# A share of the first MLP beside attention: one weight group in the second batch, both from the third on, at another pace

## The chip, the cores and the metric

The kernel runs on one core of one Trainium2 chip. The metric is device time in microseconds (us) of one execution. Engines: PE is the matmul engine (PEld its weight loads), DVE, ACT and POOL are the vector, scalar and general engines, SP issues the DMAs.

## The reference

Attention with rotary positions over 4 batches of 8 heads, 576 tokens, head size 64, then two MLPs of width 2048 over the 2304 tokens of width 512. The second MLP differs only in its activation, `s * relu(h)**2 + b`.

```python
attn = softmax(rotate(q) @ rotate(k).T / 8); x = attn @ v
h = x @ w_in
g = np.where(h >= 1, h, np.where(h <= -1, 0.0, (h + 1) ** 2 / 4))
x = g @ w_out
```

## The kernel before, in words

Every product is made of three matmuls on operands split into a high and a low part (hi*hi, hi*lo, lo*hi).

**Attention** runs in units: 16 head pairs (4 per batch) of 9 units, 144 units numbered n from 0. A unit is a block of scores (L300), its negated maximum on DVE (L302), its exponential on ACT (L305), transposes on PE (L318, L330) with casts and subtractions (L320, L324), and, behind four of a pair's nine units, the product with v (`av`). Transposes run 2 units behind the scores, `av` 4 behind. One step of the loop at L518 traces, in this order: scores, loads and rope of the next pair, transposes, `av`, and then a share of other work, `do_fill`.

**That share** is the generator `beside` (L401). Its work items are (c, gi): c is a chunk of 288 tokens (two to a batch, 0 to 4 are done here, `FC`), gi one of two groups of four slices of the 2048 hidden columns of the first MLP (`set_a`, 8 of its 16 slices). One item is four h groups (12 matmuls of 128x288 and the activation `act1`, L162) and four y groups (12 matmuls, a copy `ys` at L421, a store to `yd`). After each group it yields 1.0. It first loads and splits x of the chunk (`split_x`, four loads, casts on ACT, subtractions on POOL) and then yields `LEAD` = 4 times without work. `run_fill` (L453) adds a budget per step, `RATE` = 0.67, and takes groups while the budget is positive. A new list of items is added when a batch's last pair is finished, at n = 39, 75 and 111 (L506 to L512): [(0,0), (1,0), (0,1), (1,1)], [(2,0), (2,1), (3,0), (3,1)] and [(4,0), (4,1)]. Together they are 80 groups and three LEADs, 92 yields. What is left at the end of attention is traced behind it (L524).

**Weights** come as 64-bit words. A slice (L101) has two halves of 512 columns: the first holds its part of w_in (used by h), the second its part of w_out (used by y). `half` (L107) turns one half into a high and a low part: a load (wraw), ACT L125, DVE L126 to L129, ACT L130 (the high part), POOL L88 twice two instructions (the low part). Its stages `wa` and `wm` have one buffer each, so conversions go one behind the other. `convert` (L446) makes the next of `pending`, which lists the 16 halves of `set_a` slice by slice; it is called when n % 4 == 0 from n = 8 to 32 (`CA`), 7 times, and then when n % 3 == 0 (`CB`). `beside` also makes what is missing: both halves ahead of a slice's h (L409).

**Behind attention** come five stages (L619 to L623). The first does chunks 5 to 7 with `set_a` and makes the 16 halves of `set_b`, the second needs those. Its x is split by `split_in(0)` (L556 to L559). The change touches no line of the stages.

The order on each engine is not the order of the trace alone: for the part up to L524 a planner with its own time model puts the instructions of each engine in order at build time (program order is the priority), and on the chip each engine runs its queue strictly in that order. In the stages PE's order is that of the program.

The lines that matter below:

```python
406            grp = set_a[gi * G1:(gi + 1) * G1]
409                while sl.made < 2:
410                    sl.half(wst, WB)
444    pending = [sl for sl in set_a for _ in range(2)]
488        if n > 5 and (n % CA == 0 if n < 36 else n % CB == 0):
515        run_fill(RATE)
```

Of the kernel before, what the change touches and what calls it, by code (L numbers as in the profile page):

```python
# [24 lines left out]
NP = H // 2  # L25
KD = DM // P
NF = DFF // P
GA = 8
G1 = 4
WB = 1  # L30
# [10 lines left out]
YP = 4  # L41
N2 = 464
LEAD = 4
RATE = 0.67
CA = 4
LT = 2
LA = 4
PB = 3
YB = 4
P2 = 100  # L50
CB = 3
M1 = False
CF = None
FC = 5
# [8 lines left out]
def kernel(ctx, tc, qq, kk, vv, tab, ww1, ww2, s, b, out):  # L63
# [26 lines left out]
    def split(dst_hi, dst_lo, src, hi_eng, lo_eng):  # L90
        if hi_eng is nc.scalar:
            nc.scalar.copy(dst_hi, src)  # L92
        else:
            hi_eng.tensor_copy(dst_hi, src)
        tt = pool_tt if lo_eng is nc.gpsimd else nc.vector.tensor_tensor
        tt(out=dst_lo, in0=src, in1=dst_hi, op=ALU.subtract)  # L96
# [39 lines left out]
    def accumulate(out_ps, terms, chain=None):  # L136

        n = len(terms)
        with ExitStack() as st:
            if chain in chains:  # L140
                st.enter_context(tc.issue_after(chains[chain]))
            for i, (l, r) in enumerate(terms):
                m = nc.tensor.matmul(out_ps, l, r, start=(i == 0), stop=(i == n - 1))  # L143
        if chain is not None:
            chains[chain] = m.ins

    def h_terms(w, xh, xl):
        t = []
        for c in range(KD):
            wh, wl = w[:, 0, c * P:(c + 1) * P], w[:, 1, c * P:(c + 1) * P]  # L150
            t += [(wh, xh[:, c, :]), (wh, xl[:, c, :]), (wl, xh[:, c, :])]
        return t

    def y_terms(ws, gs, d):
        t = []
        for w, (gh, gl) in zip(ws, gs):
            o = 512 + d * P
            wh, wl = w[:, 0, o:o + P], w[:, 1, o:o + P]
            t += [(wh, gh), (wh, gl), (wl, gh)]
        return t  # L160

    def act1(ps, n, pool, gpool, lo_eng):  # L162
        c = pool.tile([P, n], F32, tag="ac", name="ac", bufs=AC)
        nc.vector.tensor_scalar(out=c, in0=ps, scalar1=-1.0, scalar2=1.0, op0=ALU.max, op1=ALU.min)
        nc.scalar.activation(c, c, AF.Square, bias=0.5, scale=0.5)
        nc.vector.tensor_tensor(out=c, in0=c, in1=ps, op=ALU.max)
        gh = gpool.tile([P, n], F32R, tag="gh", name="gh")
        gl = gpool.tile([P, n], F32R, tag="gl", name="gl")
        split(gh, gl, c, nc.scalar, lo_eng)
        return gh, gl  # L170
# [14 lines left out]
    wst = ctx.enter_context(tc.tile_pool(name="wst", bufs=1, side="right", reuse_waits="tile"))  # L185
    set_a = [Slice(wpa, ww1, f) for f in range(GA)]
# [25 lines left out]
    def load_qk(i, nm, pieces=WHOLE):  # L212
        bb, hp = divmod(i, NP)
        t = att2.tile([P, 2, S], F32, tag="qkin", name=f"{nm}in", bufs=3)
        for c in pieces:
            nc.sync.dma_start(out=t[:, :, c], in_=(qq if nm == "q" else kk)[bb, hp, :, :, c])
        qk_in[nm, i] = t

    def load_v(i):
        bb, hp = divmod(i, NP)  # L220
        t = att2.tile([P, 5, 2, D], F32, tag="vin", name="vin")
        nc.sync.dma_start(out=t, in_=vv[bb, hp])
        v_in[i] = t
# [11 lines left out]
    def rope_pair(i, nm, eng, lo_eng, pieces=WHOLE):  # L235

        t = qk_in.pop((nm, i))
        hi, lo = t[:, 0, :].bitcast(F32R), t[:, 1, :].bitcast(F32R)
        for c in pieces:
            tt = pool_tt if eng is nc.gpsimd else nc.vector.tensor_tensor  # L240
            tt(out=t[:, :, c], in0=t[:, :, c], in1=tab_sb[:, :, c], op=ALU.mult)
            r = t[:, 1, c]
            tt(out=r, in0=t[:, 0, c], in1=r, op=ALU.add)
            if nm == "q":
                nc.scalar.activation(hi[:, c], r, AF.Copy, scale=0.125)
                nc.vector.scalar_tensor_tensor(out=lo[:, c], in0=r, scalar=0.125, in1=t[:, 0, c], op0=ALU.mult, op1=ALU.subtract)
            else:
                nc.scalar.copy(hi[:, c], r)
                pool_tt(out=lo[:, c], in0=r, in1=t[:, 0, c], op=ALU.subtract)
        parts_t[nm, i] = t  # L250
        if i > 0:
            stack(i, nm, 0)
            stack(i, nm, 1)
# [15 lines left out]
    def v_pair(i):  # L269
        t = v_in[i]  # L270
        vs = att2.tile([P, 5, 4, D], F32R, tag="vs", name="vs")
        nc.scalar.copy(vs[:, :, 0::3, :], t)
        pool_tt(out=vs[:, :, 1:3, :], in0=t, in1=vs[:, :, 0::3, :], op=ALU.subtract, dim=1)
        vs_t[i] = vs
# [117 lines left out]
    def split_x(c):  # L392
        xh = m1.tile([P, KD, N1], F32R, tag="xh", name="xh")
        xl = m1.tile([P, KD, N1], F32R, tag="xl", name="xl")
        for k in range(KD):
            xs = m2.tile([P, N1], F32, tag="xs", name="xs", bufs=1)
            nc.sync.dma_start(out=xs, in_=xd[k, :, c * N1:(c + 1) * N1])
            split(xh[:, k, :], xl[:, k, :], xs, nc.scalar, nc.gpsimd)
        return xh, xl

    def beside(work):  # L401
        x = split_x(work[0][0])
        for _ in range(LEAD):
            yield 1.0
        for n, (c, gi) in enumerate(work):
            grp = set_a[gi * G1:(gi + 1) * G1]
            gs = []
            for sl in grp:
                while sl.made < 2:  # L409
                    sl.half(wst, WB)  # L410
                ps = ps_f.tile([P, 512], F32, tag="bank", name="h")
                accumulate(ps[:, :N1], h_terms(sl.w, *x), CF)
                gs.append(act1(ps[:, :N1], N1, ac1, g1p, nc.vector if c < GE else nc.gpsimd))
                yield 1.0
            if n + 1 < len(work) and work[n + 1][0] != c:
                x = split_x(work[n + 1][0])
            for d in range(KD):
                ps = ps_f.tile([P, 512], F32, tag="bank", name="y")
                accumulate(ps[:, :N1], y_terms([sl.w for sl in grp], gs, d), CF)
                y = m2.tile([P, N1], F32, tag="ys", name="ys")  # L420
                nc.scalar.copy(y, ps[:, :N1])  # L421
                nc.sync.dma_start(out=yd[gi, d, :, c * N1:(c + 1) * N1], in_=y)
                yield 1.0
# [17 lines left out]
    units = [(i, k) for i in range(NPAIR) for k in range(9)]  # L441
    fill = []
    done = 0.0
    pending = [sl for sl in set_a for _ in range(2)]

    def convert():  # L446
        while pending:
            sl = pending.pop(0)
            if sl.made < 2:
                sl.half(wst, WB)  # L450
                break

    def run_fill(budget):  # L453
        nonlocal done
        done += budget
        while fill and done > 0:
            try:
                done -= next(fill[0])
            except StopIteration:
                fill.pop(0)  # L460
        if not fill:
            done = 0.0
# [9 lines left out]
    def do_load(n):  # L472
        if n < len(units):
            i, k = units[n]
            if i + 1 < NPAIR:
                if k == 0:
                    load_qk(i + 1, "k")
                elif k == 1:
                    rope_pair(i + 1, "q", nc.gpsimd, nc.vector)
                elif k == 3:  # L480
                    rope_pair(i + 1, "k", nc.gpsimd, nc.gpsimd)
                elif k == 5:
                    load_v(i + 1)
                elif k == 7:
                    v_pair(i + 1)
                    if i + 2 < NPAIR:
                        load_qk(i + 2, "q")
        if n > 5 and (n % CA == 0 if n < 36 else n % CB == 0):
            convert()

    def do_t(n):
# [8 lines left out]
    def do_av(n):  # L500
        if n >= LA:
            i, k = units[n - LA]
            if k in AVS:
                av(i, *AVS[k])
            if k == 8:
                finish_pair(i, *rbs.pop(i))  # L506
                if (i + 1) % NP == 0 and i // NP < B - 1:
                    c = 2 * (i // NP)
                    order = [(c, 0), (c + 1, 0), (c, 1), (c + 1, 1)] if c == 0 else [(c, 0), (c, 1), (c + 1, 0), (c + 1, 1)]
                    order = [o for o in order if o[0] < FC]  # L510
                    if order:
                        fill.append(beside(order))  # L512

    def do_fill(n):
        run_fill(RATE)

    acts = {"q": do_qk, "l": do_load, "t": do_t, "a": do_av, "f": do_fill}
    for n in range(len(units) + LA):  # L518
        with ExitStack() as st:
# [156 lines left out]
```

## Time and profile before

| | us |
|---|---|
| three runs: median (lowest to highest) | 1220.44 (1219.37 to 1221.54) |
| the profiled execution: its time | 1221.28 |
| its span, first to last instruction | 1219.5 |
| PE busy in the span | 1111.2 (91%) |
| DVE, ACT, POOL busy | 790.0, 606.7, 602.6 |
| mean granted clock of PE | 0.977 |

How to read it: the span is cut into stretches below. In each, the busy time of an engine is set against the stretch, and where PE is not busy the waits and the chain say for whom it waits. PE's granted clock is a mean over the stretch between two levels, 1.2 GHz (0.5) and 2.4 GHz (1.0).

### The profile page before, as it was taken

Reading aid. Unit: us, or ns where it says so; the run is one execution under the profiler, and the core shown is the slowest. Engines: PE = TensorE matmul, PEld = TensorE weight load, DVE = VectorE, ACT = ScalarE, POOL = GpSimd, SP = SyncE. Lnnn points to the kernel's source line nnn. Section 1 sums busy time; section 2 is a strip of 40 time slices with the busy share of each in tenths; the row PEclk is TensorE's granted clock in tenths of the full one; section 3 lists DMA queues with packets and bytes.
Section 4 is the critical chain, followed back from the end, with each engine's and each line's share of the span. In section 5 each row is a group of like instructions: output and inputs, shape, how many; then the busy total and the mean of one; then the engine's idle time right before and its main releaser. Section 6 shows DMA issues by size and latency. Waiting matters only on the chain.

```text
span 1219.5 us, 19127 instructions
## 1 busy us (share of the span) xinstructions
PE 1111.2 (91%) x6628; PEld 1029.7 (84%) x6628; DVE 790.0 (65%) x1363; ACT 606.7 (50%) x1315; POOL 602.6 (49%) x778
## 2 busy tenths in 40 slices
PE   2987778859999999999979989999999999999998
PEld 2676677749998999999979889999888889988887
DVE  4787888868898777467766676677863333434443
ACT  3786667747877776455443444444443233322221
POOL 6878776875644301256677888466641101110100
PEclk9899889989999999999989999999999999999999
DMA  8766654535554401243334545442421101212210
GB/s 234 199 183 180 184 160 127 178 118 167 164 145 133 119 30 60 87 136 114 113 100 147 157 144 157 141 130 85 157 69 62 32 32 63 83 43 63 71 61 34
DMA packets 75840, 142.09 MB, mean 117 GB/s; under 512 B 12000, under 2 KB 49376, under 8 KB 75744
## 3 DMA queue, kind: packets, MB, share of 16 engines
q1 hardware_dynamic: 75744, 140.88, 39.0%
q8 instruction: 52, 0.85, 0.3%
q14 instruction: 44, 0.36, 0.1%
HBM read 90.70 MB, written 26.54 MB: 96 GB/s over the span
## 4 chain that ended last, share of the span: by engine, by line
PE 57%; POOL 13%; DVE 9%; DMA 8%; issue 7%; ACT 5%; SPq 1%; POOLq 0%; ACTq 0%; DVEq 0%
PE hps L143 21%; PE yps L590 7%; PE yps L589 7%; PE yps L591 7%; PE av L143 4%; PE sc L143 4%; PE y L143 3%; POOL wm L88 3%; POOL w L88 3%; PE tp L318 2%; DMA xs<-xd 2%; POOL xl L88 2%; POOL kin L88 2%; DMA qs<-qin 2%; PE h L143 2%
## 5 line engine op out<-in xcount | busy, mean ns | idle before, releaser
L143 PE MATMUL hps<-xh,w 128*128 128x464 f32 (+5 forms) x1216 | 347.1, 350 | 8.6 <-ACT w L130 6.1
L88 POOL TENSOR_TENSOR xl<-xs,xh 128x232 fp32r<-128x232 f32 (+5 forms) x168 | 127.0, 780 | 282.4 <-ACT xh L92 282.2
L143 PEld LDWEIGHTS hps<-xh,w 128*128 128x128 f32 x1216 | 223.2, 189 | 24.6 <-ACT w L130 6.4
L589 PE MATMUL yps<-gh,w 128*128 128x464 f32 (+5 forms) x608 | 213.7, 351 | 9.3 <-ACT yo L596 5.8
L590 PE MATMUL yps<-gl,w 128*128 128x464 f32 (+5 forms) x608 | 212.9, 350 | 0.8 <-DVE gl L96 0.7
L591 PE MATMUL yps<-gh,w 128*128 128x464 f32 (+5 forms) x608 | 212.7, 350 | 0.0
L143 PE MATMUL hps<-xl,w 128*128 128x464 f32 (+5 forms) x608 | 212.4, 349 | 0.0
L88 POOL TENSOR_TENSOR wm<-wm,w 128x256 f32<-128x256 f32 x128 | 116.6, 932 | 149.3 <-ACT w L130 66.2
L143 PE MATMUL sc<-kh,qs 128*128 128x288 f32 x320 | 102.2, 334 | 43.7 <-ACT p L305 26.9
L175 DVE TENSOR_TENSOR ar<-ar,hps 128x464 f32<-128x464 f32 (+1 forms) x80 | 50.6, 632 | 132.7 <-ACT ar L174 132.7
L302 DVE TENSOR_REDUCE nm<-sc 128x1 f32<-128x576 f32 x144 | 108.0, 751 | 39.9 <-PE sc L143 38.8
L589 PEld LDWEIGHTS yps<-gh,w 128*128 128x128 f32 x608 | 114.9, 189 | 19.9 <-ACT yo L596 8.1
L590 PEld LDWEIGHTS yps<-gl,w 128*128 128x128 f32 x608 | 114.9, 189 | 8.8 <-DVE gl L96 1.3
L143 PEld LDWEIGHTS hps<-xl,w 128*128 128x128 f32 x608 | 114.9, 189 | 7.6
L591 PEld LDWEIGHTS yps<-gh,w 128*128 128x128 f32 x608 | 115.0, 189 | 7.5
L305 ACT ACTIVATE p<-sc,nm 128x576 f32<-128x576 f32 x144 | 106.8, 744 | 18.1 <-DVE nm L302 13.2
L143 PEld LDWEIGHTS sc<-kh,qs 128*128 128x128 f32 x320 | 64.0, 200 | 52.8 <-ACT p L305 34.2
L324 DVE TENSOR_TENSOR ptl<-tp,pth 128x512 fp32r<-128x512 f32 x134 | 90.4, 682 | 27.1 <-ACT pth L320 26.4
L174 ACT ACTIVATE ar<-hps 128x464 f32<-128x464 f32 (+1 forms) x80 | 44.2, 553 | 124.7 <-PE hps L143 124.4
L88 POOL TENSOR_TENSOR w<-wm,wa 128x256 fp32r<-128x256 f32 x128 | 99.4, 794 | 0.0
L318 PE MATMUL tp<-ident,p 128*128 128x128 f32 x576 | 90.0, 283 | 7.5 <-DVE ptl L324 6.1
L96 DVE TENSOR_TENSOR gl<-ac,gh 128x288 fp32r<-128x288 f32 (+3 forms) x112 | 75.5, 675 | 28.6 <-ACT gh L92 27.5
(85 smaller groups left out, 2287.7 us busy)
## 6 DMA issues: line engine op xcount, KB each, us to landing
wraw<-in_ww SPq DMA_DIRECT2D x64, 512.0 KB, 3.7
kh<-kin SPq DMA_DIRECT2D x64, 144.0 KB, 2.7
qs<-qin SPq DMA_DIRECT2D x64, 144.0 KB, 2.6
qin<-in_q SPq DMA_DIRECT2D x15, 576.0 KB, 5.1
kin<-in_k SPq DMA_DIRECT2D x15, 576.0 KB, 3.9
xs<-y1d SPq DMA_DIRECT2D x32, 232.0 KB, 2.5
xs<-xd SPq DMA_DIRECT2D x40, 144.0 KB, 2.4
yd<-ys SPq DMA_DIRECT2D x40, 144.0 KB, 1.9
```

Source lines behind the costliest of these rows:

```text
L88: nc.gpsimd.tensor_tensor(out=out[c], in0=in0[c], in1=in1[c], op=op)
L96: tt(out=dst_lo, in0=src, in1=dst_hi, op=ALU.subtract)
L143: m = nc.tensor.matmul(out_ps, l, r, start=(i == 0), stop=(i == n - 1))
L174: nc.scalar.activation(r, ps, AF.Relu)
L175: nc.vector.tensor_tensor(out=r, in0=r, in1=ps, op=ALU.mult)
L302: nc.vector.tensor_reduce(out=nm, in_=sc[:, :, :288], axis=AX.XY, op=ALU.max, negate=True)
L305: nc.scalar.activation(p, sc[:, :, :288], AF.Exp, bias=nm, scale=1.0, accum_out=sums_t[i][:, col:col + 1])
L318: nc.tensor.transpose(v[:, c, :], p_t[i, k][:, c * P:(c + 1) * P], ident)
L324: nc.vector.tensor_tensor(out=lo, in0=v, in1=hi, op=ALU.subtract)
L589: nc.tensor.matmul(acc, wh, gh, start=f == 0, stop=False)
L590: nc.tensor.matmul(acc, wh, gl, start=False, stop=False)
L591: nc.tensor.matmul(acc, wl, gh, start=False, stop=last)
```

## The change

Five things. The lists of the items become [(0,0), (1,0)] at n = 39, [(1,1), (0,1), (2,0), (2,1), (3,0), (3,1)] at n = 75 and [(4,0), (4,1)] at n = 111: the same ten items, the two of group 1 for the first batch's chunks moved from the first list to the second. The pace is 0.55 a step up to n = 75 and 0.95 from n = 76. From n = 36 on a half is converted every 5 steps, not every 3. `pending` now has, for each group of four slices, their four first halves and then their four second halves. And `beside` makes only the first half ahead of an h, and the second halves ahead of the group's y.

```diff
-RATE = 0.67
-CB = 3
+CB = 5
...
             for sl in grp:
-                while sl.made < 2:
+                while sl.made < 1:
                     sl.half(wst, WB)
...
                 x = split_x(work[n + 1][0])
+            for sl in grp:
+                while sl.made < 2:
+                    sl.half(wst, WB)
             for d in range(KD):
...
-    pending = [sl for sl in set_a for _ in range(2)]
+
+    pending = [sl for gi in range(GA // G1) for _ in range(2) for sl in set_a[gi * G1:(gi + 1) * G1]]
+    ORDERS = [[(0, 0), (1, 0)], [(1, 1), (0, 1), (2, 0), (2, 1), (3, 0), (3, 1)], [(4, 0), (4, 1)]]
...
-        if n > 5 and (n % CA == 0 if n < 36 else n % CB == 0):
+        if n > 5 and n % (CA if n < 36 else CB) == 0:
             convert()
...
-                    c = 2 * (i // NP)
-                    order = [(c, 0), (c + 1, 0), (c, 1), (c + 1, 1)] if c == 0 else [(c, 0), (c, 1), (c + 1, 0), (c + 1, 1)]
-                    order = [o for o in order if o[0] < FC]
-                    if order:
-                        fill.append(beside(order))
+                    fill.append(beside(ORDERS[i // NP]))
...
-        run_fill(RATE)
+        run_fill(0.55 if n < 18 * NP + LA else 0.95)
```

## Rows read from the trace of the kernel before

**Rows 1.** The page, part 2: the span in 40 slices of 30.5 us, PE's busy tenths.

```profile
PE   2987778859999999999979989999999999999998
...
PEclk9899889989999999999989999999999999999999
```

**Rows 2.** Windows, line L302 alone: window, length, DVE busy (count, one a unit).

```profile
18.50:115.50 97.00, 27.34 (x37) 0.95 0.74 202
115.50:142.90 27.40, 6.68 (x9) 0.87 0.61 166
142.90:244.10 101.20, 20.23 (x27) 0.95 0.54 158
...
115.50:290.90 175.40, 33.59 (x45) 0.91 0.53 155
```

**Rows 3.** Windows, all engines: PE, PEld, DVE, ACT, POOL busy, clock, DMA share, GB/s.

```profile
18.50:115.50 97.00, 77.20 (x480) 63.38 (x480) 72.38 (x119) 68.81 (x160) 78.92 (x103) 0.95 0.74 202
115.50:142.90 27.40, 21.58 (x139) 19.79 (x139) 21.19 (x37) 19.21 (x44) 20.80 (x25) 0.87 0.61 166
142.90:244.10 101.20, 83.15 (x570) 76.00 (x568) 87.05 (x150) 68.52 (x160) 74.94 (x92) 0.95 0.54 158
...
115.50:290.90 175.40, 136.07 (x917) 125.41 (x917) 141.75 (x247) 115.02 (x266) 124.86 (x153) 0.91 0.53 155
...
290.90:516.00 225.10, 214.49 (x1629) 207.30 (x1627) 171.32 (x328) 156.16 (x379) 83.75 (x111) 1.00 0.38 108
516.00:619.00 103.00, 93.20 (x663) 91.71 (x663) 70.75 (x137) 49.18 (x108) 63.73 (x80) 0.98 0.38 117
```

**Rows 4.** Windows, line L165 alone (one an h group), then L421 (one a y group).

```profile
142.90:244.10 101.20, 3.45 (x8) 0.95 0.54 158
...
115.50:290.90 175.40, 5.22 (x12) 0.91 0.53 155
...
142.90:244.10 101.20, 3.09 (x8) 0.95 0.54 158
...
115.50:290.90 175.40, 4.60 (x12) 0.91 0.53 155
```

**Rows 5.** Windows, line L130 alone (one a converted half).

```profile
115.50:142.90 27.40, 1.24 (x2) 0.87 0.61 166
142.90:244.10 101.20, 4.37 (x7) 0.95 0.54 158
```

**Rows 6.** Waits of PE, 100 to 300 us: total, times, longest.

```profile
PE h L143 <- ACT w L130: 12.2, 1, 12.2
```

**Rows 7.** The chain that ended last, 236 to 285 us: start, length, what.

```profile
248.43 4.03 POOL kin L88 x3
...
262.57 1.38 POOL w L88 x2
...
281.59 1.59 PE y L143 x12
```

**Rows 8.** Windows, tile hps on PE alone (the stages' h matmuls): window, length, busy.

```profile
290.90:516.00 225.10, 8.70 (x48) 1.00 0.38 108
```

**Rows 9.** ACT in order of time, 480 to 530 us: start, length, line, instruction.

```profile
484.22 0.43 ACT L92 CAST xh<-xs 128x288 fp32r<-128x288 f32 x1 [0.22 <-DVE u L385]
...
515.68 0.40 ACT L421 COPY ys<-y 128x288 f32<-128x288 f32 x1 [0.81 <-PE y L143]
515.98 0.62 ACT L130 CAST w<-wm 128x512 fp32r<-128x512 f32 x1
```

**Rows 10.** POOL in order of time, 480 to 530 us.

```profile
496.41 0.81 POOL L88 TENSOR_TENSOR xl<-xs,xh 128x288 fp32r<-128x288 f32 x1 [0.75 <-ACT xh L92]
```

**Rows 11.** Waits of PE, 590 to 640 us: total, times, longest.

```profile
PE hps L143 <- ACT w L130: 6.1, 1, 6.1
```

**Rows 12.** Windows of 20 us, all engines, columns as in Rows 3.

```profile
160.00:180.00 20.00, 17.09 (x94) 15.85 (x94) 15.27 (x28) 13.33 (x33) 13.27 (x17) 0.76 0.68 194
```

**Rows 13.** The page, part 6: DMA issues, count, KB each, median us to landing.

```profile
xs<-xd SPq DMA_DIRECT2D x40, 144.0 KB, 2.4
```

## The prediction

> **What bounds the kernel now.** I read the page's slices first [rows 1]: PE reads 9 of 10 nearly everywhere from the eleventh slice (305 us) on. It is loose in the first nine (to 275 us), worst in the ninth, and once more in the twentieth and twenty-first (580 to 640 us); in both places its mean granted clock is below 1.00 [rows 3]. As the change adds and removes no matmul, only these stretches have time to give.
>
> Next come the units of attention [rows 2] and the engines beside them [rows 3]. The 36 units of the first batch take 97.0 us, 24.3 per pair of nine. The next pair, without any MLP group yet but with two converted halves [rows 5], takes 27.4. The three pairs after it, with 8 h and 8 y groups [rows 4] and seven halves [rows 5], take 101.2, or 33.7 each. The fifth pair takes the rest of the 175.4 us for these 45 units (36 to 80). PE is busy for 136.07 of the 175.4, 78%; DVE for 141.75, 81%. No engine is full: this is a stretch of waits in fixed queues. From 290.9 us to the end of the MLP share at 516 PE is busy for 214.49 of 225.1, 95%, with the full clock: PE is the bound there.
>
> The waits of PE name the largest loose piece: one h group waited 12.2 us for a converted half [rows 6]. The chain of that stretch shows why. A half's last step on POOL (w L88, at 262.57) stood behind the rope of the next pair (kin, at 248.43) [rows 7], and the next half could begin only after it. The waiting h belongs to item (0,1), so to group 1, whose halves were called by unit 60 and came while units 72 to 80 ran (262.57 lies behind 244.1, where unit 72 begins); behind that h on PE's queue stood the scores, transposes and av of attention.
>
> The last reading is the seam behind attention. The first half of the next eight slices is written by ACT at 515.98, right behind the last `ys` copy of the share at 515.68 [rows 9]. Sixteen halves follow, and PE waits for the late ones, 6.1 us in its longest wait [rows 11], until about 619. So in the 103 us from 516 to 619, where PE is busy 93.2 [rows 3], the conversions are the bound, and they start when the share ends. **What counts is when the share ends.**
>
> **Part by part.** *Units 36 to 80.* Before, 12 h and 12 y groups are done there [rows 4]; after, the first list only, 16 groups. The nine halves left at unit 36 stay nine, but the last is called at unit 80 instead of 60. The price of a group beside attention: (33.7 - 27.4) us a pair, over 16 groups in 3 pairs, is 1.19 us. New time: 5 x 27.4 + 16 x 1.19 = 156.0 us, 19.4 less than 175.4. Of this, 9.5 us are eight groups moved away and 9.9 the stall of 12.2, net of what ran under it. Bounds: at the first batch's pace 45 units take 121.3, with the groups 140.3 (35.1 less); with groups at their full 1.59 us on PE [rows 7] it is 162.4 (13.0 less). I take 19.4, from the nearest pairs.
>
> *From unit 81 to the end of the share.* The eight groups come back, 8 x 1.59 = 12.7 us, now where PE is the bound. Out goes what PE did of the first stage in this stretch, 48 recorded matmuls [rows 8] of 1.59/12 us, 6.4, because less of the share is left to mix with it. The budget shows how much: 72 steps of 0.95 give 68.4 of the 72 yields left, so about 4 groups remain behind attention; before, 109 steps of 0.67 gave 73 of 92, so 19 remained. PE's idle time is 10.6 us (225.1 - 214.49); with nearly one group ready per unit I take 6.6, with 0 and 21 (twice as much) as bounds. Sum: +12.7 - 6.4 - 4.0 = +2.3 (-4.3 to +16.9).
>
> *The seam.* Splitting the first stage's x takes from 484.22 on ACT [rows 9] to 497.2 on POOL [rows 10], 13.0 us, hidden now by 19 groups. With 4 groups left, 6.4 us, up to 6.6 us of PE are uncovered. The conversions run on beside it, and PE has room: 93.2 plus the 6.4 us moved in makes 99.6 of 103, 3.4 free. I take +2 (0 to 6.6).
>
> *Moved at no cost, with their cover.* The eight groups take with them 8 loads of x (144 KB, 2.4 us to landing [rows 13]), their casts and POOL subtractions and 8 stores. They pass on SP's queue from a stretch with a DMA share of 0.53 to one of 0.38, and on POOL from 71% to 37% busy [rows 3]. If that cover failed, a late x would hold one h for a landing, 2.4 us. The halves come every 5 units, about 17 us, where the chip needed about 14 (101.2 us for seven [rows 5]); their loads pass only behind rope loads of later pairs. The new place of the second halves, ahead of y, adds a wait in y: behind it on PE stand the scores and av of the next units. It is priced as a rival.
>
> **Sum**, against the profiled execution of 1221.28 us: -19.4 + 2.3 + 2.0 = -15.1, so 1206.2. That execution lies 0.84 above the median of the runs, so I forecast **1205.3 us**. All lower bounds together give -39, all upper ones +10.5; half way to each of them is the forecast's own range, 1194 to 1218.
>
> **The rivals.** *The wait moves to y* (0.17). The last second half of group 1 is called at unit 80, and the first y of item (1,1) needs it: 4 empty yields and 4 h groups at 0.95 from unit 76 put that at about unit 84. Four units are about 13 us, one conversion; halves came over ten units late before. If it is late, PE waits there instead, half to all of 12.2 us: 1211 to 1217.
>
> *Slower: attention cannot feed PE at 0.95 a unit* (0.13). From unit 81 on each unit's scores, transposes and av share four PSUM banks and the DVE queue with nearly one group. If PE's share fell from 95% to 88.6%, half way to the 82% of units 45 to 71 (83.15 of 101.2 [rows 3]), the 220.8 us of PE work would take 249.2 instead of 227.4: +21.8, 1227. It decides the sign from 91% down (15 us lost). Against it: DVE was busy 76% of that stretch, POOL 37%, and the lower share of units 45 to 71 came with seven conversions, which are then over.
>
> *The clock* (0.04). Where PE had gaps, its granted clock was lower: 0.76 in 160 to 180 us [rows 12], 0.91 over units 36 to 80, 0.95 in the first batch without any group [rows 3]. With fewer groups beside units 36 to 80 the gaps could grow. At 0.76 instead of 0.91 the 123.4 us of PE work left there (136.07 - 12.7) would take 20% more, +24: 1229. The first batch, at 80% busy and 0.95, speaks against it, for the forecast has 123.4 of 156, 79%. The Trainium skill, "TensorE: Matmul & The Clock Gate", section "What's actually happening", says that "the default state is throttled, and activity releases the throttle". By that rule thinning the work would cost clock; the trace agrees in direction, and not in size.
>
> *It changes nothing* (0.08). The planner orders by its own clock, and halves or groups may land where they were: 1220.4.
>
> **How the numbers follow.** The forecast has 0.58, the rivals 0.17, 0.13, 0.04 and 0.08. About 0.2% (2.4 us) is what a measurement of this kernel can tell from no change. Faster: 0.58 + 0.17 = 0.75; slower: 0.13 + 0.04 = 0.17; same: 0.08. The range 1193 to 1222 holds the forecast, the moved wait and no change, 0.83, less some 0.03 for a larger gain; the slower cases lie outside.
>
> **What would show it.** Unit 81 near 271 us instead of 290.9, no wait of ten us for a converted half in PE's waits before 300 us, and 16 groups by then, of group 0 alone. The share's last `ys` copy near 499, PE at 97% between, some 4 groups behind the last av. The first half of the next slices right behind that copy, and 103 us from there to the last wait for them. I am wrong if pairs five to nine still take over 165 us, if y waits for L130 or POOL w at unit 84, if PE's share after unit 81 is below 91%, or if the start of that conversion moves and the end of the kernel does not.

## The result, and the profile after

The changed kernel takes 1205.53 us (median of four runs, 1203.56 to 1207.65), the kernel before, on the same chip, 1220.99 (1219.37 to 1225.53). The ratio is 0.9868, with a 95% interval of 0.9836 to 0.9899: 1.3% faster, 15.5 us. The forecast was 1205.3. The profiled execution took 1205.45 us, its span 1203.6. The changed kernel's line numbers are lower by 1 up to the generator, so its L301 is L302 of before, and its `ys` copy is L423.

The units first (windows of the changed kernel with line L301 alone: window, length, DVE busy and count, then clock, DMA share, GB/s), beside [rows 2]:

```profile
117.00:146.30 29.30, 6.67 (x9) 0.86 0.59 159
...
117.00:259.50 142.50, 33.74 (x45) 0.96 0.60 169
```

Units 36 to 80 take 142.5 us instead of 175.4. The window closes just behind the maximum of unit 81, which starts at 258.3 us instead of 290.0. The engines in these stretches and in the 103 us behind the seam, beside [rows 3] (columns PE, PEld, DVE, ACT, POOL):

```profile
117.00:259.50 142.50, 117.95 (x834) 109.57 (x833) 126.47 (x221) 105.11 (x246) 111.11 (x137) 0.96 0.60 169
259.50:501.00 241.50, 227.13 (x1684) 219.92 (x1683) 181.10 (x344) 161.16 (x388) 97.29 (x124) 0.97 0.39 111
500.00:603.00 103.00, 98.78 (x702) 96.43 (x700) 76.93 (x148) 53.18 (x119) 65.74 (x80) 1.00 0.41 124
```

PE is busy 83% of units 36 to 80 instead of 78%, and its clock is 0.96 instead of 0.91. From unit 81 to the share's end it is busy 94%, no better than before, and the stretch is longer: 241.5 us against 225.1. Cut finer, the loose part is at its beginning:

```profile
275.00:295.00 20.00, 16.85 (x93) 15.45 (x92) 14.17 (x24) 11.17 (x25) 15.79 (x20) 0.74 0.67 165
295.00:315.00 20.00, 16.66 (x116) 15.94 (x115) 14.39 (x27) 12.88 (x32) 12.99 (x17) 0.91 0.38 124
315.00:336.00 21.00, 20.44 (x157) 19.76 (x157) 14.72 (x29) 14.73 (x37) 4.53 (x7) 1.00 0.50 136
...
336.00:501.00 165.00, 160.08 (x1228) 156.55 (x1227) 123.36 (x237) 112.15 (x273) 51.68 (x68) 1.00 0.33 95
```

Only 93 and 116 matmuls run in the first two stretches of 20 us, 157 in the third. From 336 us on PE is busy 97%, which was the forecast for the whole stretch.

PE's waits from 100 to 300 us (total, times, longest), beside [rows 6]; no wait for a converted half (ACT w) is among them:

```profile
PE sc L142 <- ACT p L304: 18.9, 12, 4.7
PE y L142 <- DVE ptl L323: 2.6, 3, 1.2
PE av L142 <- DVE ptl L323: 2.2, 3, 1.0
```

The seam, ACT in order of time, beside [rows 9]:

```profile
499.63 0.40 ACT L423 COPY ys<-y 128x288 f32<-128x288 f32 x1 [0.89 <-PE y L142]
499.93 0.62 ACT L129 CAST w<-wm 128x512 fp32r<-128x512 f32 x1
...
501.10 0.40 ACT L423 COPY ys<-y 128x288 f32<-128x288 f32 x1
```

The next slices' first half is written at 499.93, 16.05 us earlier than 515.98; the last copy of the share follows it at 501.10. The span is 15.9 us shorter. The rest is a constant: 1219.5 - 515.98 = 703.5 us before, 1203.6 - 499.93 = 703.7 us after. It is not PE's work that makes it one: from there to the end PE is busy 681.5 us before and 686.3 after, because fewer matmuls of the first stage were done ahead of the seam.

### The profile page after: what moved, and what is told of

It is laid out like the page before. It is cut to its first block, busy times and chain, and to the rows that moved or that the text cites. A ratio compares the mean times of both kernels' runs of the same rounds, so it can differ in the third digit from the quotient of the medians.

```text
span 1203.6 us, 19127 instructions
## 1 busy us (share of the span) xinstructions
PE 1109.6 (92%) x6628; PEld 1030.7 (86%) x6628; DVE 792.4 (66%) x1363; ACT 604.5 (50%) x1315; POOL 608.5 (51%) x778
## 4 chain that ended last, share of the span: by engine, by line
PE 48%; DVE 16%; POOL 14%; DMA 9%; issue 7%; ACT 6%; SPq 1%; POOLq 0%; ACTq 0%; DVEq 0%
PE hps L142 15%; PE yps L589 5%; PE yps L591 5%; PE yps L590 5%; POOL w L87 5%; POOL wm L87 4%; PE sc L142 4%; PE av L142 3%; PE y L142 3%; PE h L142 3%; DMA xs<-xd 3%; POOL xl L87 3%; PE tp L317 3%; DVE wm L126 2%; DVE nm L301 2%
## 5 line engine op out<-in xcount | busy, mean ns | idle before, releaser
L87 POOL TENSOR_TENSOR xl<-xs,xh 128x232 fp32r<-128x232 f32 (+5 forms) x168 | 131.5, 807 | 256.5 <-ACT xh L91 256.3
L301 DVE TENSOR_REDUCE nm<-sc 128x1 f32<-128x576 f32 x144 | 108.2, 752 | 40.0 <-PE sc L142 38.4
L304 ACT ACTIVATE p<-sc,nm 128x576 f32<-128x576 f32 x144 | 106.9, 745 | 19.3 <-DVE nm L301 15.3
L319 ACT CAST pth<-tp 128x512 fp32r<-128x512 f32 x134 | 77.7, 585 | 39.5 <-PE tp L317 38.9
L142 PE MATMUL sc<-kz,qs 128*128 128x288 f32 x320 | 95.1, 311 | 0.0
```

Source lines behind the costliest of these rows:

```text
L87: nc.gpsimd.tensor_tensor(out=out[c], in0=in0[c], in1=in1[c], op=op)
L301: nc.vector.tensor_reduce(out=nm, in_=sc[:, :, :288], axis=AX.XY, op=ALU.max, negate=True)
L304: nc.scalar.activation(p, sc[:, :, :288], AF.Exp, bias=nm, scale=1.0, accum_out=sums_t[i][:, col:col + 1])
L319: nc.scalar.copy(hi, v)
```

## The experiments

Each run gives a ratio to the kernel before on the same chip, whose medians were 1217 to 1220 us. "Chain start" is the ACT instruction at which the first of the second eight slices' 16 halves is written (499.93 in the last fence). A trace is one execution, and its times scatter more than the ratios do: in the trace of "short before" below, the longest of ten executions, unit 72 begins 8 us later than in the kernel before (250.4 against 242.6), though up to there PE, DVE, ACT and POOL run the same instructions in the same order in both.

**The parts by themselves.** Pace alone, on the kernel before:

```diff
-        run_fill(RATE)
+        run_fill(0.55 if n < 18 * NP + LA else 0.95)
```

> The kernel before with the new pace alone (0.55 to n = 75, then 0.95), old lists, old conversions. My theory: the gain comes from when the groups run, and this pace puts the same 16 groups ahead of n = 75 and leaves about 4 behind attention, so nearly all of the gain is here: 1205 to 1209 us, unit 81 before 270 us, no wait of PE over 6 us for a converted half before 300 us. Rival (the late halves are the cause, the pace only spreads work): the wait stays, 1215 to 1221.

Measured: 1213.46 us, ratio 0.9949 (0.9929 to 0.9969). PE's waits from 100 to 300 us:

```profile
PE h L143 <- ACT w L130: 11.4, 1, 11.4
PE sc L143 <- ACT p L305: 9.8, 7, 3.4
```

A miss on both sides: unit 81 is early (its maximum starts at 260.2 us) and half of the gain is there, but the wait for group 1's half is there too: (0,1) is still third in the first list, and by the budget its first h is traced at about unit 75.

Lists alone, on the kernel before: the three lists of the change, 0.67 throughout, halves as before.

```diff
...
-                    order = [(c, 0), (c + 1, 0), (c, 1), (c + 1, 1)] if c == 0 else [(c, 0), (c, 1), (c + 1, 0), (c + 1, 1)]
...
+                    fill.append(beside(ORDERS[i // NP]))
```

> The kernel before with the new lists alone, 0.67 throughout. My theory: the stall for group 1's half goes and units 36 to 80 shorten as in the change (unit 81 near 262 us), but only 69 of 92 yields are taken by the end of attention, so some 23 groups stand behind it and the share ends near 508: 1210 to 1215 us. Rival (PE is not the bound behind unit 81 and the pace is of no account): 1205 to 1208.

Measured: 1212.24 us, ratio 0.9935 (0.9918 to 0.9952), inside my range. This run prices the stall. Units 72 to 80, from maximum to maximum, in the kernel before and then in this run:

```profile
242.60:290.00 47.40, 31.08 (x209) 28.91 (x208) 34.12 (x64) 27.35 (x64) 30.16 (x37) 0.86 0.48 144
```

```profile
242.80:264.60 21.80, 18.32 (x127) 16.79 (x126) 21.16 (x39) 16.99 (x39) 19.59 (x26) 0.92 0.61 185
```

It reaches unit 72 when the kernel before does, to 0.2 us; unit 81 then starts at 264.6 instead of 290.0. Eight groups and one wait, 8 x 1.59 + 12.2 = 24.9 us, left these nine units, and the nine units became 25.6 us shorter. PE's busy time fell by 12.8 us and its idle time by 12.8 (from 16.3 to 3.5): the groups at their full time on PE and the stall in full.

Conversions alone, on the kernel before: every 5 units, first halves first.

```diff
-CB = 3
+CB = 5
...
-                while sl.made < 2:
+                while sl.made < 1:
...
```

> The kernel before with the new order and spacing of conversions alone (first halves first, every 5 units), old lists and pace. My theory: the wait of 12.2 us for a first half goes or becomes a shorter one for a second half, the 24 groups by unit 81 stay: 1211 to 1217 us. Rival (the stall is the whole gain): 1204 to 1208. Rival (the conversions are of no account, the wait only moves): 1219 to 1223.

Measured: 1228.62 us, ratio 1.0096 (1.0063 to 1.0129): slower than every theory. PE's waits from 100 to 300 us:

```profile
PE y L143 <- POOL w L88: 8.4, 4, 6.4
PE y L143 <- ACT w L130: 3.6, 2, 3.1
```

The 12.2 us of h became 12.0 us of y, for second halves. Unit 81 does begin 18 us earlier (271.9 against 290.0), with four y groups fewer done by then (20 groups, not 24), but from there to the chain start it takes 248.0 us instead of 226.0, and the chain start moves from 515.98 to 519.96. So by itself this part only moves the wait, and an early unit 81 alone is worth nothing.

Lists and pace together, without the conversions' part:

> The change without its conversion part (halves slice by slice, every 3 units). My theory: group 1 is wanted only from unit 80 on, when halves made every 3 units are ready, so 1204 to 1209 us and no long wait for a half. Rival (the conversions' order and spacing carry the gain): a wait of PE for a half of over 6 us comes back, 1212 to 1220.

Measured: 1205.22 us, ratio 0.9888 (0.9858 to 0.9917). The whole change has 0.9868 (0.9836 to 0.9899); the intervals lie on one another. The two gains, 8.0 and 6.8 us, add to 14.8 of the 15.0 measured here. The conversions' part brings nothing that these runs can tell; one wait of h of 4.6 us stands in this run's trace, and none in the changed kernel's.

Earlier calls of the halves, on the kernel before (`CA = 3` for 4):

> The kernel before with halves made every 3 units instead of every 4 in the first batch (9 by unit 33, the last called at n = 54 instead of 60); lists, pace and slice order as before. My theory: the stall of PE for group 1's half is a fault of its own; with the halves earlier it goes, unit 81 comes 10 to 20 us earlier with the same 24 groups done: 1205 to 1212 us. Rival (the halves cost their time wherever they stand, units 0 to 35 lengthen by as much): 1217 to 1222.

Measured: 1221.78 us, ratio 1.0040 (1.0022 to 1.0058). The rival's number, but not by its mechanism: the last halves of `set_a` are written at the same place as before (265.2 and 271.1 us against 266.5 and 272.2) and PE waits the same 12.2 us. In the traces PE, DVE, ACT and POOL run the same instructions in the same order as in the kernel before; of 606 DMA issues one load of a half moved ahead by two places. The planner undid the edit, so the run tries neither earlier halves nor a stall-free kernel with 24 groups; both stay open. It shows instead that two kernels so nearly equal can differ by 0.4% here, outside the interval, so differences of that size between runs are not read as effects.

**The seam.** The halves of `set_b` made shorter, in both kernels; the 29 low bits of those weights are left out.

```diff
+            brief = self.ww is ww1 and self.f >= GA
...
+            if brief:
+                pool_tt(out=lo, in0=m, in1=hi, op=ALU.subtract)
+                return
```

> The kernel before with a shorter conversion of the 16 halves of the first stage: two of four DVE steps and one of two POOL steps are left out (the 29 low bits of those weights are dropped), some 1.5 us less per half in the chain. My theory for before: from the share's end to the second stage the chain of conversions is the bound, so the 8.6 us that PE waits there go: 1211 to 1215 us. Rival (PE is the bound from the share's end on): 1218 to 1222.

> The changed kernel with the same shorter conversion. My theory: the chain is still the last to wait for, but PE's waits for it are only 3.7 us there, so 2 to 4 us: 1201 to 1204. Rival (the chain binds as before, PE follows it): 8 us or more, 1198 or less. Rival (PE alone binds now): 1205 to 1207.

Measured: 1208.55 us, ratio 0.9917 (0.9892 to 0.9942), and 1192.85 us, ratio 0.9799 (0.9784 to 0.9814). Both gain more than I had expected, for I had priced the shorter conversion at 1.5 us less per half: in the changed kernel the first half is written at 499.93 and the sixteenth at 608.86, with the shorter conversion at 495.76 and 559.54, which is 3.0 us less per half. From the chain start to the end the two runs need 687.4 and 693.5 us instead of 703.5 and 703.7. So the chain of conversions binds behind the share in both kernels, and what PE waits for it there, 8.6 us before (6.1 [rows 11] and 2.5 for POOL) and 3.7 after (the two lines below), does not show all of it: with the shorter chain PE is busy 102.52 us of the first 103, with the full one 98.78. Both shorter versions and the next one also take work off POOL (busy 65.74 us of these 103), so the length of the chain and the load of POOL are not told apart.

```profile
PE hps L142 <- POOL w L87: 2.5, 1, 2.5
PE hps L142 <- ACT w L129: 1.2, 1, 1.2
```

```profile
496.00:599.00 103.00, 102.52 (x736) 101.84 (x735) 74.25 (x145) 60.39 (x135) 57.69 (x77) 1.00 0.51 154
```

The first fence is PE's waits of the changed kernel from 590 to 640 us, the second a window of it with the shorter chain.

A version that does the same work, on lists and pace: the first of the two POOL steps of `set_b`'s halves on DVE.

```diff
-            pool_tt(out=m, in0=m, in1=hi, op=ALU.subtract)
+            tt = nc.vector.tensor_tensor if self.ww is ww1 and self.f >= GA else pool_tt
+            tt(out=m, in0=m, in1=hi, op=ALU.subtract)
```

> The kernel with the new lists and pace and the old conversions, and for the first stage's 16 halves the first of the two POOL steps done on DVE in one instruction, the result the same: about 0.7 us on DVE for two of 0.93 us on POOL, some 1 us less per half in the chain. My theory: the chain of conversions binds from the share's end to the second stage, 16 halves by 1 us less as far as PE has idle time there, 6 to 10 us: 1195 to 1200 us. Rival (DVE, three quarters busy there, delays act1 and takes it back): 1203 to 1208.

Measured: 1196.20 us, ratio 0.9810 (0.9782 to 0.9839): faster than the kernel before and than lists and pace, on which it stands (0.9888); the interval just touches that of the whole change (0.9836 to 0.9899). The two lines are the step on POOL (in the other 48 halves) and on DVE (in the 16) in this run (count, busy us, mean ns, idle before); the window is PE's first 103 us behind the seam:

```profile
L88 POOL TENSOR_TENSOR wm<-wm,w 128x256 f32<-128x256 f32 x96 | 83.9, 895 | 88.5 <-DVE wa L128 42.2 <-ACT w L130 32.3 <-issue 10.3
L132 DVE TENSOR_TENSOR wm<-wm,w 128x512 f32<-128x512 f32 x16 | 12.0, 750 | 6.5 <-ACT w L130 6.5
...
500.00:603.00 103.00, 102.85 (x738) 102.39 (x737) 88.82 (x172) 56.70 (x126) 46.10 (x59) 1.00 0.43 131
```

A half's two POOL instructions took 2 x 895 ns, the one on DVE 750: 1.04 us less per half. DVE is busy 86% there and takes nothing back that shows; PE is now full, and the end comes 695.3 us behind the chain start. The Trainium skill, "GPSIMD Engine Reference", section "4.1 Engine selection", gives POOL as about twice as slow as DVE for operations of two inputs. Here it is 2.4 times.

**The pace.** 0.85 and 1.05 for the change's 0.95, and 0.85 with the first eight steps of the first stage at no priority.

```diff
-        run_fill(0.55 if n < 18 * NP + LA else 0.95)
+        run_fill(0.55 if n < 18 * NP + LA else 0.85)
```

> The changed kernel at 0.85 instead of 0.95 a unit from n = 76: 61 of 72 yields by the end of attention, so some 11 groups behind it instead of 4. My theory: PE is the bound from unit 81 on, so where the groups stand is of no account as long as PE is full; the share ends within 3 us of 501: 1204 to 1208 us. Rival (attention cannot feed PE at 0.95, so a slower pace is better): 1198 to 1202. Rival (0.95 is needed): 1209 or more.

> The changed kernel at pace 0.85 with no priority for the first eight steps of the first stage: on PE 13 of that stage's matmuls, not 48, stand ahead of the share's last y. My theory: the conversions start with the share's end and bind from there, so what PE does for the stage before that end only delays it: 35 x 0.1325 = 4.6 us earlier, 1208 to 1211 us against 1214. Rival (the 11 groups left behind attention are the cause): 1213 to 1216.

> The changed kernel at 1.05 instead of 0.95 a unit: nothing of the share is left behind the last av and no matmul of the first stage stands ahead of its end. My theory: PE is the bound from unit 81 on, the share and attention end together, up to 1 us earlier than now, and the conversions start there: 1203 to 1207 us. Rival (attention cannot feed PE at that pace): 1209 or more. Rival (the uncovered split of the first stage's x now counts): 1208 to 1212.

Measured: 1214.22 us, ratio 0.9957 (0.9934 to 0.9980); 1211.60, 0.9937 (0.9910 to 0.9964); 1211.03, 0.9935 (0.9910 to 0.9960). My theory missed at both ends: 0.95 is the best of the three paces. At 0.85 the chain start is 511.03, 11 us later. 48 of the first stage's matmuls are recorded ahead of the share's end instead of 11, as in the kernel before; taking the priority away brings the start to 508.45, but the intervals of the two overlap, so this cause is likely and not settled, and most of the 11 us is not explained by it. At 1.05 the share ends first (last `ys` copy at 491.8), and yet the start is 499.41, no earlier than with 0.95: on ACT it stands behind the first cast of the first stage's x, whose load is issued only when attention's last matmul is done (495.9). So in this run not the share's end holds the chain but attention's end and that load. From there the end takes 707.9 us, for PE waits for the split of x that no share covers (that cast and the chain start on ACT, then PE's waits from 485 to 640 us):

```profile
499.07 0.43 ACT L91 CAST xh<-xs 128x288 fp32r<-128x288 f32 x1 [2.83 <-DMA xs<-xd]
499.41 0.61 ACT L129 CAST w<-wm 128x512 fp32r<-128x512 f32 x1
```

```profile
PE hps L142 <- ACT xh L91: 4.0, 2, 3.6
PE hps L142 <- POOL xl L87: 1.1, 3, 0.5
```

So the four groups that 0.95 leaves are the cover of that split, and the uncovered seam that I priced at 2 us is what a faster pace pays (707.9 for 703.7).

**The late halves.** The shorter conversion for the eight halves of group 1 in the changed kernel (`brief` for slices 4 to 7; the 29 low bits of those weights are left out).

> The changed kernel with the shorter conversion for the eight halves of group 1 alone (two DVE and one POOL step left out, the 29 low bits of those weights dropped). What it asks: why the stretch from unit 81 to the share's end took 241 us and not 227. My theory: three late halves hold DVE and POOL in units 81 to 98 (PE idle 9.4 us, clock 0.91 in 259 to 336 us of the changed kernel); shortened, the second halves are in time, that idle time falls to 5 us or less and the share ends 3 to 6 us earlier: 1199 to 1203 us. Rival (the chain of scores and exponentials makes that idle time): 1204 to 1207.

Measured: 1193.58 us, ratio 0.9774 (0.9743 to 0.9804), twice what I expected. The changed kernel's first 76.5 us behind the maximum of unit 81, then the same length from the same unit in this run, and there the whole stretch to the last `ys` copy:

```profile
259.50:336.00 76.50, 67.06 (x458) 63.38 (x457) 57.74 (x108) 49.00 (x116) 45.61 (x56) 0.91 0.52 144
```

```profile
260.60:337.10 76.50, 73.54 (x555) 70.67 (x554) 59.53 (x113) 52.56 (x131) 45.09 (x58) 1.00 0.49 145
260.60:488.00 227.40, 220.00 (x1677) 213.98 (x1677) 170.86 (x328) 156.15 (x383) 87.05 (x112) 1.00 0.38 108
```

555 matmuls run in 76.5 us instead of 458, at full clock. The eight cheaper halves are all ready by 252 us, so none is converted behind unit 81 any more: that they come earlier and that they take less of DVE and POOL are not told apart. The first `ys` copy of item (1,1) is at 277.9 us instead of 295.32, and the chain starts at 486.76, 13.2 us earlier. In the changed kernel the last second half is ready on POOL at 294.6, only just ahead of that first copy:

```profile
293.17 1.42 POOL L87 TENSOR_TENSOR w<-wm,wa 128x256 fp32r<-128x256 f32 x2
```

What PE did for these y groups in the meantime (windows of the changed kernel with tile y alone: window, length, PE busy and count, clock, DMA share, GB/s):

```profile
275.00:280.00 5.00, 3.29 (x16) 0.66 0.30 88
280.00:285.00 5.00, 1.22 (x8) 1.00 0.82 189
285.00:290.00 5.00, 0.68 (x2) 0.56 0.64 133
290.00:295.00 5.00, 3.17 (x21) 0.76 0.92 248
```

In order of time 24 of the item's 48 y matmuls have begun by 281.8, two come at 288.2, one at 291.1, and 21 from 292.3 on. This is how three accumulations look that have eight of their twelve matmuls, get the ninth when the low part of slice 6 is there (286.4), and end with slice 7. Each holds one of the four PSUM banks that transposes and av also need. In order of time, PE's transposes wait there for the last reader of the transposes ahead of them and then, in its longest wait from 259.5 to 336 us, for the copy of a y group:

```profile
285.67 0.64 PE L329 MATMUL tr<-ident,p 128*64 128x128 f32 x2 [1.59 <-DVE ptl L323]
...
301.55 0.41 PE L329 MATMUL tr<-ident,p 128*64 128x128 f32 x2 [2.73 <-ACT ys L423]
```

A transpose and that copy have only a bank in common. That the banks are what thins attention in the whole stretch is read from these rows; no run gives y banks of its own.

**All profiled runs in one rule.** Span less chain start, in us: before 703.5, after 703.7, pace alone 704.7, lists alone 703.4, conversions alone 703.9, lists and pace 703.9, early halves 703.1, 0.85 702.0 and 701.2, short group 1 705.0. The chain start itself goes from 486.8 to 520.0. Only the runs that touch the seam leave the rule: 1.05 (707.9), the two shorter chains (687.4 and 693.5) and the step on DVE (695.3). Of these, 687.4 is from the long execution named above.

## Why the prediction was right

The time was right to 0.2 us and the mechanism (what counts is when the share ends) was right, but two terms were mis-sized in opposite directions, by 13.5 and 13.0 us. That they cancel so closely is luck.

*Units 36 to 80*, forecast -19.4: -32.9 measured (142.5 for 175.4). Two prices were too low. I took a group beside attention at 1.19 us and the stall at 9.9 "net of what ran under it"; lists alone shows 1.59 and 12.2, nothing net, for behind a waiting h nothing else of PE's queue ran. That is 24.9 instead of 19.4. The rest, some 8 us, goes with the slower pace, to which I had given no term of its own; pace alone, with two y groups fewer done by then, has unit 72 at 231.1 us instead of 242.6.

*From unit 81 to the share's end*, forecast +2.3: +15.3 (240.4 us to the chain start for 225.1). The eight groups came back and the stage's matmuls left, as worked out: 11 are recorded there for 48. The step that failed is "with nearly one group ready per unit I take 6.6" of idle time: it is 14.4 (241.5 - 227.13). PE's busy time is over too, 227.13 for the 220.8 forecast: 1.5 us are the 11 matmuls that stayed, and the rest goes with a clock of 0.97 for 1.00, 0.74 at its worst. The groups were not ready. This is the rival of the wait that moves to y, which I had priced at 6 to 12 us with a chance of 0.17: the second halves were late. Short group 1 shows what they cost: without them the stretch takes 227.4 us (226.2 to the chain start), the length of the forecast, with 7.4 idle and 220.0 busy. I looked for it as a wait of PE; it came as a hole of the plan. The planner had put other work between the parts of the y groups, so no wait of PE names the halves, while the open groups, as I read the rows, kept three of four banks.

*The seam*, forecast +2: +0.2. "103 us from there to the last wait" was nearly right: the last wait ends 105.2 us behind the chain start, 102.9 before, and PE did 5.6 us more in the first 103 (98.78 for 93.20). With 1.5 us that unit 36 begins later: -32.9 + 1.5 + 15.3 + 0.2 + 0.1 (outside the span) = -15.8, the difference of the two profiled executions.

*The rivals.* PE's share behind unit 81 is 94%, above the 91% that I had set as the sign's limit. The clock over units 36 to 80 rose to 0.96 instead of falling: the pace had taken groups away, but the gap of 12 us was gone too; no run separates the two. Where it fell, PE had been loose just before (windows of the changed kernel with PE alone; 0.66 and 0.56 are means of 5 us that were partly at 1.2 GHz):

```profile
270.00:275.00 5.00, 2.90 (x24) 1.00 0.26 59
275.00:280.00 5.00, 5.00 (x29) 0.66 0.30 88
280.00:285.00 5.00, 3.29 (x25) 1.00 0.82 189
285.00:290.00 5.00, 3.57 (x13) 0.56 0.64 133
```

By the rule of the Trainium skill ("TensorE: Matmul & The Clock Gate", "What's actually happening") it is activity that releases the clock; the trace agrees with it in these four rows, where PE is busy 2.90 and 3.29 of 5 us ahead of the two lower clocks.

*A reading.* The second loose place on the page is the 21st slice alone (610 to 640 us), not the twentieth; no term rests on it.

*Unpredicted:* the conversions' order and spacing, three of the change's five edits, are of no measurable account here and harmful alone.

## What to carry to other kernels

Find the event behind which everything is a constant, here the start of one serial chain of 16 conversions, and score each edit by when it lets that event happen, not by an earlier milestone such as unit 81. A stall on an in-order queue was worth its whole length here and the moved work its full time; do not net one against other engines' work without a row that shows it. When a planner fixes the queues, look for late data also where no wait shows it, in stretches with few matmuls, and try it by making the late work cheaper.

## What the runs showed that I had not expected

A chain that shows 3.7 us of waits on PE (changed kernel, behind the seam) was worth some 10: with it shortened the end came 693.5 us behind its start instead of 703.7, and the ratios differ by 8 us. A pace changed by a tenth of a group per unit, down or up, cost 11 and 8 us by the ratios. And an edit of when a conversion is called (`CA = 3`) changed the place of one load and nothing else.
